# Weighting attention probabilities in the transpose: diagonal matrices in place of gate transposes, and a mask on row pairs

## The chip, the cores and the metric

The kernel runs on one core of one Trainium2 chip. The metric is device time in microseconds, from runs of the whole program. The core has five engines that work from queues of their own: PE (TensorE: matrix products; its weight loads are listed as PEld), DVE (VectorE), ACT (ScalarE), POOL (GpSimd) and SP, which here issues DMAs. Matrix products are written to PSUM, eight banks of 128 partitions by 512 f32 numbers; all else lies in SBUF.

## The reference, cut to what matters

Two blocks, one after the other. The first is a linear attention with polynomial features (4 batches, 4 heads, 1088 positions, head size 32). Its output, with the heads side by side, is `x` of the second: 4 batches of 1088 rows of 128 numbers. The second is a mixture of four attention experts, and the change lies there:

```python
logits = x @ w_gate                       # four experts per row
topk = np.argpartition(-logits, 2)[:2]    # the two best; w = softmax over these two
for e in range(4):
    q, k, v = x @ wq[e], x @ wk[e], x @ wv[e]          # 64 columns each
    scores = where(causal, -1e9, q @ k.T / 8)
    a = exp(scores - scores.max(-1)); a /= a.sum(-1) + 1e-9
    ye = a @ v @ wo[e]
    out += (w of this row for expert e, or 0) * ye
```

Everything is computed in f32. All four experts are computed for all rows; the gate `w` is zero for the two that a row does not choose. So a row of an expert's `a` is multiplied by two numbers, its gate and one over its sum of exponentials, and it makes no difference in the result whether that is done to `a` or to `a @ v`.

## The kernel before

**Tiling.** Keys and queries are cut into blocks of 128 rows (eight, and a ninth of 64). Experts go in pairs `g` (two). A *unit* is one block of queries `i`, one batch `b` and one pair `g`: 8 x 2 x 4 = 64 units, and four more of kind "L" for the last 64 rows of each batch, which hold both pairs at once. Two units with neighbouring blocks ("A" and "B", x = 0 and 1) share one tile of transposed weights `aT` and one product with the values.

**One unit**, in the order of its data:

1. `scores` (L367; `scores_last`, L393): PE forms q k^T for both experts of the pair in two groups of 64 array rows (L379), and adds the causal mask on the last 128 columns by a bf16 product of the identity with a mask matrix (L382; in the last unit L412). DVE takes the row maximum (L386 for up to 512 keys, both experts in one instruction; else L389, one each). ACT takes the exponential into the tile `a` and sums it into `z` (`soften`, L364).
2. `turns_of` (L427): PE transposes `a` block by block against the f32 identity (L434), four blocks to one PSUM bank `tp`, and `evacuate` (L67) copies the bank into `aT`: every third evacuation on DVE (L70), the others on ACT (L72). The blocks come in the order of keys, with the two experts next to each other.
3. `gates` (L443): DVE adds 1e-9 to the sums and takes the reciprocal (L446, L447); POOL multiplies by the gate and spreads the product over 64 columns for each expert, `rb` (L450); PE transposes `rb` (L457) into `rt`, and ACT copies that into `rs` (L459). This is done for two units together.
4. `values` (L491; L519 in the last unit): PE multiplies `aT` by the values (L497, L526); DVE multiplies the result by `rs` on its way from PSUM into `yT` (L499, L528).
5. `output` (L535): PE multiplies `yT` by `wo` (L540), the result is evacuated, and SP writes it out.

**What sets the order.** PE's order is written out by hand: everything from L548 on is traced under a manual schedule of that one engine. The driver at the end of the function goes through the units. The work of a unit that waits for ACT is put off: after the scores of a unit come the transposes of the unit before (`jobs`), then pieces of the preparation of the next batch (`fill`, given out by `spend`), and then, where a unit has more than two banks of transposes, the first half of its own; its other banks become `jobs` of the next unit. The gate turn goes into the jobs of an "A" unit, the values behind the scores of a "B" unit, the output into the jobs of a later unit. On DVE, ACT, POOL and SP the order is left to a planner that takes instructions by readiness and order of tracing.

**Preparation.** `prepare` (L193) makes a batch's `x`, the projections of queries, keys and values, and the gates `gw` (the last 64 rows also as `gw8`). Constants are made at the start: the identity `ident` on POOL, its bf16 copy `identb` on DVE (L169), the mask `cmask` on POOL (L171).

**PSUM.** Four of the eight banks belong to the scores (two tiles `sc` of two banks); the other four turn round under the tag `tp`: transposes, values, gate turns, output and all of the preparation.

Of the kernel before, what the change touches and what calls it, by code (L numbers as in the profile page):

```python
# [19 lines left out]
def kernel(  # L20
# [46 lines left out]
    def evacuate(out_, in_):  # L67
        turn[0] += 1
        if turn[0] % 3 == 0:
            nc.vector.tensor_copy(out_, in_)  # L70
        else:
            nc.scalar.copy(out_, in_)  # L72
# [95 lines left out]
    identb = const("identb", [128, 128], BF16)  # L168
    nc.vector.tensor_copy(identb, ident)  # L169
    cmask = const("cmask", [128, 128], BF16)  # L170
    make_causal_mask(nc, cmask, mask_val=-1e30)  # L171
# [195 lines left out]
    def scores(b, i, g, qk, z):  # L367

        n = 128 * i + 128
        if n <= 512:  # L370
            t = ps_sc.tile([128, 2, 512], F32, tag="sc", name=f"sc{b}_{i}_{g}")
            sc = [t[:, e, :] for e in range(2)]
        else:
            sc = [ps_sc.tile([128, 1024], F32, tag="sc", name=f"sc{b}_{i}_{g}_{e}") for e in range(2)]
        for c0 in range(0, n, 512):
            c1 = min(c0 + 512, n)
            for e in range(2):
                rows = slice(64 * e, 64 * e + 64)
                nc.tensor.matmul(sc[e][:, c0:c1], qk[rows, g, 128 * i : 128 * i + 128], qk[rows, NG + g, c0:c1],  # L379
                                 start=True, stop=(c1 < n))  # L380
        for e in range(2):
            nc.tensor.matmul(sc[e][:, 128 * i : n], identb, cmask, start=False, stop=True)  # L382
        mx = p4.tile([128, 2], F32, tag="mx", name=f"mx{b}_{i}_{g}")
        ats = [p4.tile([128, S], F32, tag="a", name=f"a{b}_{i}_{g}_{e}") for e in range(2)]
        if n <= 512:
            nc.vector.tensor_reduce(mx, t[:, :, 0:n], axis=AX.X, op=ALU.max, negate=True)  # L386
        for e in range(2):
            if n > 512:
                nc.vector.tensor_reduce(mx[:, e : e + 1], sc[e][:, 0:n], axis=AX.X, op=ALU.max, negate=True)  # L389
            soften(ats[e][:, 0:n], sc[e][:, 0:n], mx[:, e : e + 1], z[:, e : e + 1])  # L390
        return ats

    def scores_last(b, qk, z):  # L393
# [16 lines left out]
        for e in range(2):  # L410
            for g in range(NG):
                nc.tensor.matmul(ext[e][64 * g : 64 * g + 64], identb[:, 0:64], cmask[:, 0:64],  # L412
                                 start=False, stop=True)
        ats = []
        for e in range(2):
            mx, zz = (p4.tile([128, 2], F32, tag=t, name=f"{t}{b}_8_{e}") for t in ("mx", "zz"))
            nc.vector.tensor_reduce(mx[:, 0:1], sc[e], axis=AX.X, op=ALU.max, negate=True)
            nc.vector.tensor_reduce(mx[:, 1:2], ext[e], axis=AX.X, op=ALU.max, negate=True)
            nc.vector.tensor_tensor(out=mx[:, 0:1], in0=mx[:, 0:1], in1=mx[:, 1:2], op=ALU.min)
            a = p4.tile([128, S], F32, tag="a", name=f"a{b}_8_{e}")  # L420
            soften(a[:, 0:1024], sc[e], mx[:, 0:1], zz[:, 0:1])
            soften(a[:, 1024:], ext[e], mx[:, 0:1], zz[:, 1:2])
            nc.vector.tensor_tensor(out=z[:, e : e + 1], in0=zz[:, 0:1], in1=zz[:, 1:2], op=ALU.add)
            ats.append(a)
        return ats

    def turns_of(name, i, ats, aT, q0):  # L427

        def some(k0, k1):
            tp = ps_tp.tile([128, 4, 128], F32, tag="tp", name=f"tp{name}_{k0}")  # L430
            nk = size(k0 // 2)
            for k in range(k0, k1):
                j, e = divmod(k, 2)
                nc.tensor.transpose(tp[0:nk, k - k0, :], ats[e][:, 128 * j : 128 * j + nk], ident)  # L434
            evacuate(aT[0:nk, k0:k1, q0 : q0 + 128], tp[0:nk, 0 : k1 - k0, :])

        full = 2 * min(i + 1, NJ - 1)
        cuts = [(k, min(k + 4, full)) for k in range(0, full, 4)]
        if i == NJ - 1:
            cuts.append((full, full + 2))  # L440
        return [lambda k0=k0, k1=k1: some(k0, k1) for k0, k1 in cuts]

    def gates(name, z, gws, w):  # L443

        r = p4.tile([128, w // 128, 2], F32, tag="r", name=f"r{name}")
        nc.vector.tensor_scalar_add(r, z, 1e-9)  # L446
        nc.vector.reciprocal(r, r)  # L447
        rb = p4.tile([128, 2, 128], F32, tag="rb", name=f"rb{name}", bufs=2)
        wide = [128, w // 128, 2, HD]
        nc.gpsimd.tensor_tensor(out=rb[:, 0 : w // 128].rearrange("p x (e d) -> p x e d", d=HD),  # L450
                                in0=gws[:, :, :, None].to_broadcast(wide), in1=r[:, :, :, None].to_broadcast(wide),
                                op=ALU.mult)

        def turn():
            t = ps_tp.tile([128, 512], F32, tag="tp", name=f"rt{name}")
            for x in range(w // 128):
                nc.tensor.transpose(t[:, 128 * x : 128 * x + 128], rb[:, x], ident)  # L457
            rs = p4.tile([128, 256], F32, tag="rs", name=f"rs{name}", bufs=2)
            nc.scalar.copy(rs[:, 0:w], t[:, 0:w])  # L459
            return rs  # L460

        return turn
# [16 lines left out]
    def units(b, qk, vt, gw, gw8):  # L479


        for p in range((NJ - 1) // 2) if b < B - 1 else reversed(range((NJ - 1) // 2)):
            yT = p2.tile([128, NG, 256], F32, tag="yT", name=f"yT{b}_{p}")
            nk = 2 * (2 * p + 2)
            for g in range(NG):
                aT = p2.tile([128, 16 * 256], F32, tag="aT", name=f"aT{b}_{p}_{g}")
                aT = aT[:, 0 : nk * 256].rearrange("p (k s) -> p k s", s=256)
                z = p4.tile([128, 2, 2], F32, tag="z", name=f"z{b}_{p}_{g}")
                name = f"{b}_{p}_{g}"

                def values(rs, p=p, g=g, aT=aT, yT=yT, name=name):  # L491
                    av = ps_tp.tile([128, 512], F32, tag="tp", name=f"av{name}")
                    for j in range(2 * p + 2):
                        lo = 128 * max(0, j - 2 * p)
                        for e in range(2):
                            c = HD * (2 * g + e)
                            nc.tensor.matmul(av[HD * e : HD * e + HD, lo:256], vt[:, j, c : c + HD],  # L497
                                             aT[:, 2 * j + e, lo:256], start=(j == 0), stop=(j == 2 * p + 1))
                    nc.vector.tensor_tensor(out=yT[:, g], in0=av[:, 0:256], in1=rs, op=ALU.mult)  # L499
                    return (lambda: output(b, p, yT)) if g == NG - 1 else None  # L500

                def close(p=p, g=g, z=z, name=name, values=values):
                    return gates(name, z, gw[:, 2 * p : 2 * p + 2, 2 * g : 2 * g + 2], 256), values

                for x in range(2):
                    i = 2 * p + x
                    yield ("AB"[x], lambda i=i, g=g, z=z, x=x: scores(b, i, g, qk, z[:, x]),
                           lambda ats, i=i, aT=aT, x=x, name=name: turns_of(f"{name}_{x}", i, ats, aT, 128 * x),
                           close if x else None)
# [3 lines left out]
    def last_unit(b, qk, vt, gw8):  # L513
        aT = p2.tile([128, 16 * 256], F32, tag="aT", name=f"aT{b}_8")
        aT = aT[:, 0 : 18 * 128].rearrange("p (k s) -> p k s", s=128)
        z = p4.tile([128, 1, 2], F32, tag="z", name=f"z{b}_8")
        yT = p2.tile([128, NG, 256], F32, tag="yT", name=f"yT{b}_8")

        def values(rs):  # L519
            av = ps_tp.tile([128, 512], F32, tag="tp", name=f"av{b}_8")  # L520
            for g in range(NG):
                for j in range(NJ):
                    m = size(j)
                    for e in range(2):
                        c = HD * (2 * g + e)
                        nc.tensor.matmul(av[HD * e : HD * e + HD, 64 * g : 64 * g + 64], vt[0:m, j, c : c + HD],  # L526
                                         aT[0:m, 2 * j + e, 64 * g : 64 * g + 64], start=(j == 0), stop=(j == NJ - 1))
            nc.vector.tensor_tensor(out=yT[:, :, 0:64], in0=av[:, 0:128].rearrange("p (g s) -> p g s", g=NG),  # L528
                                    in1=rs[:, 0:128].rearrange("p (g s) -> p g s", g=NG), op=ALU.mult)
            return lambda: output(b, NJ // 2, yT)  # L530

        return ("L", lambda: scores_last(b, qk, z[:, 0]), lambda ats: turns_of(f"{b}_8", NJ - 1, ats, aT, 0),
                lambda: (gates(f"{b}_8", z, gw8[:, None, :], 128), values))
# [14 lines left out]
    with tc.manual_schedule(engines={mybir.EngineType.PE}):  # L548
# [10 lines left out]
        for b in range(B):  # L559
# [4 lines left out]
            for n, (kind, make, turned, close) in enumerate(units(b, *now)):  # L564
# [4 lines left out]
                if group and kind != "B":  # L569
                    to_gate, values = group  # L570

                    def gate_turn(to_gate=to_gate, values=values):
                        rs = to_gate()
                        return lambda: values(rs)

                    if kind == "A":
                        box = []
                        jobs.append(lambda gate_turn=gate_turn, box=box: box.append(gate_turn()))
                if kind == "L":
                    for f in jobs:  # L580
                        f()
                    values = gate_turn()
                    ats = make()
                    done = values()
# [3 lines left out]
                else:  # L588
                    ats = make()
# [9 lines left out]
                    if kind == "A" and group:  # L599
                        group = box[0]  # L600
                if n == 0 and b == 0:
                    while len(fill) > need + 5:
# [4 lines left out]
                turns = turned(ats)  # L607
# [4 lines left out]
                if close:  # L612
                    group = close()
# [4 lines left out]
        to_gate, values = group  # L618
        for f in turns + ([done] if done else []):
            f()  # L620
        values(to_gate())()
# [30 lines left out]
```

## Time and profile before

| | |
|---|---|
| median of three runs | 418.97 us (418.88 to 420.64) |
| the profiled execution | 420.57 us, of which the profile's span is 418.7 us |
| granted clock of PE | 0.995 of full speed |
| busy: PE / DVE / ACT / POOL | 396.7 / 232.1 / 224.9 / 55.9 us |
| records of PE / DVE / ACT / POOL | 3284 / 496 / 564 / 84 |
| first product of the preparation starts | 9.52 us |
| last evacuation (L72, `ob`) starts | 415.40 us |

A row of the groups reads: line, engine, operation, what it writes <- what it reads, the shapes, the number of records, and behind the bar the time in which at least one of them ran, the mean duration of one, and the engine's idle time just before them with what ended it. Matmuls are pipelined, so the durations of neighbours overlap: the mean duration is not the time from one to the next. For a matmul the shape gives the weights first (array rows * columns) and then what streams past them. A row of the timeline reads: start, length, engine, line, operation, tiles, shape and count of a burst. The idle time of an engine that does not bound the kernel costs nothing.

### The profile page before, as it was taken

Reading aid. Unit: us, or ns where it says so; the run is one execution under the profiler, and the core shown is the slowest. Engines: PE = TensorE matmul, PEld = TensorE weight load, DVE = VectorE, ACT = ScalarE, POOL = GpSimd, SP = SyncE. Lnnn points to the kernel's source line nnn. Section 1 sums busy time; section 2 is a strip of 40 time slices with the busy share of each in tenths; the row PEclk is TensorE's granted clock in tenths of the full one; section 3 lists DMA queues with packets and bytes.
Section 4 is the critical chain, followed back from the end, with each engine's and each line's share of the span. In section 5 each row is a group of like instructions: output and inputs, shape, how many; then the busy total and the mean of one; then the engine's idle time right before and its main releaser. Section 6 shows DMA issues by size and latency. Waiting matters only on the chain.

```text
span 418.7 us, 8188 instructions
## 1 busy us (share of the span) xinstructions
PE 396.7 (95%) x3284; PEld 274.1 (65%) x3284; DVE 232.1 (55%) x496; ACT 224.9 (54%) x564; POOL 55.9 (13%) x84
## 2 busy tenths in 40 slices
PE   5989999999999999998999999999999998999995
PEld 5965777865666766775765776786666565576663
DVE  5775756754854464656447345556575545545552
ACT  1325565655546464555745555575455655455662
POOL 2200460000000361000000063000000000000110
PEclk9989999999999999999999999999999999999999
DMA  8631032000000000000000000000000000000000
GB/s 201 170 104 58 0 112 65 6 8 2 13 3 15 5 0 14 2 14 0 15 1 2 14 3 14 2 12 2 2 13 2 0 14 5 2 14 4 2 13 28
DMA packets 11351, 9.98 MB, mean 24 GB/s; under 512 B 3632, under 2 KB 10288, under 8 KB 11312
## 3 DMA queue, kind: packets, MB, share of 16 engines
q1 hardware_dynamic: 9296, 8.92, 7.5%
q10 hardware_dynamic: 2016, 0.53, 0.7%
q8 instruction: 26, 0.43, 0.4%
q14 instruction: 13, 0.11, 0.1%
HBM read 7.22 MB, written 2.23 MB: 23 GB/s over the span
## 4 chain that ended last, share of the span: by engine, by line
PE 80%; ACT 9%; DVE 6%; issue 3%; DMA 1%; POOL 0%; POOLq 0%; ACTq 0%; DVEq 0%
PE sc L379 18%; PE tp L434 15%; PE av L497 14%; PE qk L304 7%; ACT a L365 6%; PE sc L382 3%; PE po L540 3%; PE num L277 3%; PE kps L229 2%; PE vg L316 2%; PE kv L255 2%; PE av L526 2%; PE tq L268 2%; PE sc L402 2%; DVE mx L389 2%
## 5 line engine op out<-in xcount | busy, mean ns | idle before, releaser
L365 ACT ACTIVATE a<-sc,mx 128x1024 f32<-128x1024 f32 (+7 forms) x136 | 103.0, 762 | 86.7 <-DVE mx L389 48.2
L434 PE MATMUL tp<-ident,a 128*128 128x128 f32 (+1 forms) x648 | 95.1, 278 | 6.3 <-ACT a L365 4.8
L389 DVE TENSOR_REDUCE mx<-sc 128x1 f32<-128x640 f32 (+3 forms) x64 | 62.6, 1019 | 49.0 <-PE sc L382 49.0
L72 ACT COPY aT<-tp 128x512 f32<-128x512 f32 (+1 forms) x122 | 63.1, 539 | 45.6 <-PE tp L434 45.2
L434 PEld LDWEIGHTS tp<-ident,a 128*128 128x128 f32 (+1 forms) x648 | 71.3, 140 | 22.4 <-ACT a L365 9.7
L379 PE MATMUL sc<-qkT 64*128 64x512 f32 (+3 forms) x384 | 80.9, 518 | 0.8 <-ACT a L365 0.8
L497 PE MATMUL av<-aT,vt 128*64 128x256 f32 (+1 forms) x640 | 69.2, 363 | 0.0
L450 POOL TENSOR_TENSOR rb<-gw,r 128x256 f32<-128x256 f32 (+1 forms) x36 | 21.2, 589 | 322.9 <-DVE r L447 258.2
L497 PEld LDWEIGHTS av<-aT,vt 128*64 128x64 f32 x640 | 42.9, 137 | 21.7 <-issue 0.2
L379 PEld LDWEIGHTS sc<-qkT 64*128 64x128 f32 x384 | 32.2, 185 | 31.3 <-issue 26.2
L70 DVE COPY aT<-tp 128x512 f32<-128x512 f32 (+2 forms) x58 | 37.7, 652 | 16.2 <-PE tp L434 15.7
L386 DVE TENSOR_REDUCE mx<-sc 128x2 f32<-128x256 f32 (+3 forms) x32 | 26.2, 819 | 19.7 <-PE sc L382 19.7
L304 PE MATMUL qk<-xT,wqk 128*128 128x512 f32 x64 | 33.0, 633 | 1.0 <-ACT xT L72 0.9
L365 ACT ACTIVATION_READ_ACCUMULATOR a<-sc,mx 128x1 f32 x136 | 27.1, 199 | 0.0
L382 PEld LDWEIGHTS <-identb 128*128 128x128 bf16 x128 | 7.3, 97 | 28.1 <-issue 26.2
L316 PE MATMUL vg<-wvg,xT 128*128 128x260 f32 (+1 forms) x72 | 21.4, 396 | 1.1 <-DVE vt L70 0.5
L540 PE MATMUL po<-wo,yT 128*128 128x128 f32 (+1 forms) x144 | 20.5, 282 | 1.7 <-ACT aT L72 0.8
L499 DVE TENSOR_TENSOR yT<-av,rs 128x256 f32<-128x256 f32 x32 | 13.5, 422 | 13.9 <-PE av L497 13.7
L540 PEld LDWEIGHTS po<-wo,yT 128*128 128x128 f32 (+1 forms) x144 | 17.5, 185 | 3.5 <-ACT aT L72 1.1
L382 PE MATMUL sc<-cmask,identb 128*128 128x128 bf16 x128 | 18.3, 224 | 0.0
L304 PEld LDWEIGHTS qk<-xT,wqk 128*128 128x128 f32 x64 | 11.1, 199 | 10.2 <-issue 5.9
L277 PE MATMUL num<-kvz,qpT 128*128 128x66 f32 x144 | 17.4, 271 | 0.0
(118 smaller groups left out, 402.3 us busy)
## 6 DMA issues: line engine op xcount, KB each, us to landing
kin<-in_k_dram SPq DMA_DIRECT2D x4, 544.0 KB, 3.7
qin<-in_q_dram SPq DMA_DIRECT2D x4, 544.0 KB, 5.5
vin<-in_v_dram SPq DMA_DIRECT2D x16, 128.0 KB, 3.4
out_dram<-ob SPq DMA_DIRECT2D x16, 128.0 KB, 1.8
wqk<-in_moe_wq_dram ACTq DMA_DIRECT2D x1, 128.0 KB, 4.3
wqk<-in_moe_wk_dram ACTq DMA_DIRECT2D x1, 128.0 KB, 6.6
wvg<-in_moe_wv_dram ACTq DMA_DIRECT2D x1, 128.0 KB, 6.8
wo<-in_moe_wo_dram ACTq DMA_DIRECT2D x1, 128.0 KB, 6.0
```

The costliest lines, as they stand in the source:

```text
L70: nc.vector.tensor_copy(out_, in_)
L72: nc.scalar.copy(out_, in_)
L277: nc.tensor.matmul(num[:, 66 * y : 66 * y + 66], qpT[:, 6 * g + y], kvz[:, y % 2].rearrange("p h d -> p (h d)"), start=True, stop=True)
L304: nc.tensor.matmul(t, wt(a), xT[:, 512 * c : 512 * c + 512], start=True, stop=True)
L316: nc.tensor.matmul(t[0:m, 0 : E * HD + E], xT[:, 128 * j : 128 * j + m], wvg, start=True, stop=True)
L365: nc.scalar.activation(out=dst, in_=src, func=ACTF.Exp, bias=mx, accum_out=z)
L379: nc.tensor.matmul(sc[e][:, c0:c1], qk[rows, g, 128 * i : 128 * i + 128], qk[rows, NG + g, c0:c1], start=True, stop=(c1 < n))
L382: nc.tensor.matmul(sc[e][:, 128 * i : n], identb, cmask, start=False, stop=True)
L389: nc.vector.tensor_reduce(mx[:, e : e + 1], sc[e][:, 0:n], axis=AX.X, op=ALU.max, negate=True)
L434: nc.tensor.transpose(tp[0:nk, k - k0, :], ats[e][:, 128 * j : 128 * j + nk], ident)
L497: nc.tensor.matmul(av[HD * e : HD * e + HD, lo:256], vt[:, j, c : c + HD], aT[:, 2 * j + e, lo:256], start=(j == 0), stop=(j == 2 * p + 1))
L540: nc.tensor.matmul(po[0:nq, DM * x : DM * x + DM], yT[:, g, 128 * x : 128 * x + nq], wo_sb[:, g], start=(g == 0), stop=(g == NG - 1))
```

## The change

- The weights `a` are no longer transposed against the identity, but multiplied, as stationary operand, by a diagonal matrix `dg` (f32, 128x128, one for each expert of a unit) with gate over sum on the diagonal. The result is the transposed and already weighted `a`. `nc.tensor.transpose` becomes `nc.tensor.matmul`.
- `weigh` makes these matrices on DVE: 1e-9 is added to the sums, the reciprocal taken, and the identity scaled by reciprocal and gate. In units with more than 512 keys and in the last unit that is done for each expert by itself, behind its exponential; in the others for both at once, when the transposes are begun.
- `gates` is dropped, and with it the broadcast on POOL, the transposes of `rb` and the copies to `rs`. `values` ends with a plain copy on ACT.
- A PSUM bank of transposes now holds blocks of one expert (for five and six blocks one bank holds the remainders of both), and `aT` is laid out by expert first.
- The mask is added in two halves of 64 columns by products over 64 array rows, a pair for the two experts: `mrows` holds a triangle of 64 rows, and `mpick` picks a row of it for each query.
- Every fourth instead of every third evacuation goes to DVE; in the first batch the loop over `fill` stops at need + 3 instead of need + 5.

```diff
     def evacuate(out_, in_):
         turn[0] += 1
-        if turn[0] % 3 == 0:
+        if turn[0] % 4 == 0:
...
-    identb = const("identb", [128, 128], BF16)
-    nc.vector.tensor_copy(identb, ident)
-    cmask = const("cmask", [128, 128], BF16)
-    make_causal_mask(nc, cmask, mask_val=-1e30)
+    mrows = const("mrows", [128, 64], BF16)
+    mpick = const("mpick", [128, 2, 128], BF16)
+    nc.gpsimd.memset(mrows, 0.0)
+    nc.gpsimd.memset(mpick, 0.0)
+    for e in range(2):
+        rows = slice(64 * e, 64 * e + 64)
+        for out_, cols, base, keep, fill in (
+            (mrows[rows], 64, 0, ALU.is_gt, -1e30),
+            (mpick[rows, 0], 128, -1, ALU.not_equal, 1.0),
+            (mpick[rows, 1, 64:], 64, -1, ALU.not_equal, 1.0)):
+            nc.gpsimd.affine_select(out=out_, in_=out_, compare_op=keep, fill=fill,
+                                    base=base, pattern=[[-1, cols]], channel_multiplier=1)
+        nc.gpsimd.memset(mpick[64 * e : 64 * e + 1, 1, 0:64], 1.0)
...
+    def sums(name):
+        z = p4.tile([128, 2], F32, tag="z", name=f"z{name}")
+        return z, p4.tile([128, 2, 128], F32, tag="dg", name=f"dg{name}", bufs=3)
+
+    def weigh(dg, z, gws, e0, e1):
+        nc.vector.tensor_scalar_add(z[:, e0:e1], z[:, e0:e1], 1e-9)
+        nc.vector.reciprocal(z[:, e0:e1], z[:, e0:e1])
+        for e in range(e0, e1):
+            nc.vector.tensor_scalar(out=dg[:, e], in0=ident, scalar1=z[:, e : e + 1], scalar2=gws[:, e : e + 1],
+                                    op0=ALU.mult, op1=ALU.mult)
...
-        for e in range(2):
-            nc.tensor.matmul(sc[e][:, 128 * i : n], identb, cmask, start=False, stop=True)
+        for half in range(2):
+            for e in range(2):
+                rows = slice(64 * e, 64 * e + 64)
+                c0 = 128 * i + 64 * half
+                nc.tensor.matmul(sc[e][:, c0 : c0 + 64], mpick[rows, half], mrows[rows], start=False, stop=(half == 1))
...
             soften(ats[e][:, 0:n], sc[e][:, 0:n], mx[:, e : e + 1], z[:, e : e + 1])
-        return ats
+            if n > 512:
+                weigh(dg, z, gws, e, e + 1)
+        return ats, dg, (lambda: weigh(dg, z, gws, 0, 2)) if n <= 512 else None
...
-        def some(k0, k1):
-            tp = ps_tp.tile([128, 4, 128], F32, tag="tp", name=f"tp{name}_{k0}")
-            nk = size(k0 // 2)
-            for k in range(k0, k1):
-                j, e = divmod(k, 2)
-                nc.tensor.transpose(tp[0:nk, k - k0, :], ats[e][:, 128 * j : 128 * j + nk], ident)
-            evacuate(aT[0:nk, k0:k1, q0 : q0 + 128], tp[0:nk, 0 : k1 - k0, :])
-
-        full = 2 * min(i + 1, NJ - 1)
-        cuts = [(k, min(k + 4, full)) for k in range(0, full, 4)]
+        def some(e0, e1, j0, j1):
+            tp = ps_tp.tile([128, 512], F32, tag="tp", name=f"tp{name}_{e0}_{j0}")
+            nk, nj = size(j0), j1 - j0
+            for e in range(e0, e1):
+                for j in range(j0, j1):
+                    x = nj * (e - e0) + j - j0
+                    nc.tensor.matmul(tp[0:nk, 128 * x : 128 * x + 128], ats[e][:, 128 * j : 128 * j + nk], dg[:, e],
+                                     start=True, stop=True)
+            evacuate(...)
+        n = min(i + 1, NJ - 1)
+        if n <= 2:
+            cuts = [(0, 2, 0, n)]
+        elif n <= 4:
+            cuts = [(0, 1, 0, n), (1, 2, 0, n)]
+        elif n <= 6:
+            cuts = [(0, 1, 0, 4), (0, 2, 4, n), (1, 2, 0, 4)]
+        else:
+            cuts = [(0, 1, 0, 4), (0, 1, 4, n), (1, 2, 0, 4), (1, 2, 4, n)]
...
-                    nc.vector.tensor_tensor(out=yT[:, g], in0=av[:, 0:256], in1=rs, op=ALU.mult)
+                    nc.scalar.copy(yT[:, g], av[:, 0:256])
...
-                    while len(fill) > need + 5:
+                    while len(fill) > need + 3:
```

`gates` and its calls in the driver are deleted; the last unit (`scores_last`, `last_unit`) is changed in the same way.

## The prediction

> **What bounds the kernel now.** I read the page's first part, its chain and its costliest groups; then the groups kept apart by shape; then the timeline of short stretches, to count matmul records against the calls in the code.
>
> ```profile
> PE 396.7 (95%) x3284; PEld 274.1 (65%) x3284; DVE 232.1 (55%) x496; ACT 224.9 (54%) x564; POOL 55.9 (13%) x84
> PE 80%; ACT 9%; DVE 6%; issue 3%; DMA 1%; POOL 0%; POOLq 0%; ACTq 0%; DVEq 0%
> ```
>
> TensorE (PE) is busy 95% of the span and makes 80% of the chain that ended last. VectorE (DVE) and ScalarE (ACT) stand still almost half of the time. So a change counts by what it does to PE's stream of matmuls, and work on DVE or ACT counts only where PE has to wait for it. PE's idle time is 418.7 - 396.7 = 22.0 us.
>
> ```profile
> L434 PE MATMUL tp<-ident,a 128*128 128x128 f32 x640 | 93.9, 278 | 6.3 <-ACT a L365 4.8 <-DVE xs L284 0.5 <-DVE aT L70 0.4
> L540 PE MATMUL po<-wo,yT 128*128 128x128 f32 x128 | 17.9, 281 | 1.7 <-ACT aT L72 0.8 <-DVE yT L499 0.5 <-DVE aT L70 0.2
> L457 PE MATMUL rt<-ident,rb 128*128 128x128 f32 x68 | 13.6, 277 | 0.9 <-POOL rb L450 0.7
> L382 PE MATMUL sc<-cmask,identb 128*128 128x128 bf16 x128 | 18.3, 224 | 0.0
> ```
>
> Line 434 holds the transposes of the attention weights. Line 540 is an ordinary f32 matmul of the same shape: 128x128 stationary, 128 columns moving. By the column of mean durations the two cost the same, 278 and 281 ns, and one would call the exchange of the one for the other free. But the durations overlap, and the counts say something else. Lines 434 and 441 ask for 162 transposes per batch, 648 in all, and the page counts 648 records at L434. Lines 538 to 541 ask for 18 matmuls per batch, 72 in all, and the page counts 144. Every other f32 matmul is doubled too: 10 calls at line 552 make 20 records, 32 projections at line 304 make 64. The transposes (also L268, L294, L457) and the bf16 mask matmuls (64 x 2 = 128) have one record per call. The timeline of PE shows it in one place:
>
> ```profile
> 406.37 0.28 PE L382 MATMUL sc<-cmask,identb 128*128 128x128 bf16 x2
> 406.49 0.61 PE L434 MATMUL tp<-ident,a 128*128 128x128 f32 x4
> 406.93 1.06 PE L540 MATMUL po<-wo,yT 128*128 128x128 f32 x8
> 407.83 0.38 PE L457 MATMUL rt<-ident,rb 128*128 128x128 f32 x2
> ```
>
> Four transposes hold the stream from 406.49 to 406.93, where the next burst starts: 0.44 us, 0.110 each. The eight records after them are one call of the output projection, two blocks by two groups, so four matmuls: 406.93 to 407.83, 0.90 us, 0.225 each. An f32 matmul takes two passes, a transpose one.
>
> **The change part by part.**
>
> Transposes become matmuls. Each of the 648 transposes against the identity becomes an f32 matmul of the same 128x128 weights against an f32 diagonal matrix. I take the price of the row with the same operands' shapes and types, L540, in a longer run of the timeline:
>
> ```profile
> 205.17 1.05 PE L540 MATMUL po<-wo,yT 128*128 128x128 f32 x8
> 207.93 1.04 PE L434 MATMUL tp<-ident,a 128*128 128x128 f32 x8
> ```
>
> Start to start, a record takes (1.05 - 0.275)/7 = 0.111 us at L540 and (1.04 - 0.272)/7 = 0.110 us at L434. So a transpose goes from 0.110 to 0.222 us, and 648 x 0.112 = **+72.6 us**, all of it on the engine that is the bound. That a diagonal is nearly all zeros takes nothing off: the matmuls of line 552 have the identity on both sides and still have two records. Ends: 0 if these matmuls went in one pass, +72.6 otherwise; I take the second, by the row.
>
> The Trainium skill, "TensorE: Matmul & The Clock Gate", section Terms, says that on trn2 the transpose mode is four times faster for FP32; this trace has a factor of 2.0 (0.222 against 0.110). By the page's factor the step would cost an estimated 648 x 3 x 0.110 = 214 us and the kernel would end near 616 us; the measured factor decides.
>
> Gate transposes and their surroundings go. 68 transposes of `rb` at 0.110 = **-7.5 us** on PE, and with them PE's wait for POOL, **-0.7 us** (the row of L457). The 36 copies of `rs` on ACT (12.4 us for 32 of them) go, and 36 copies of `yT` come in their place; the multiplications of `yT` leave DVE (13.5 us for 32). On ACT the copy stands in line behind exponentials of 1.1 us; the output projection that reads it comes only in the next unit's work, so I cost it at nothing; uncovered it would be 36 x about 0.4 = 14 us at most.
>
> Diagonals on DVE. Lines with up to 512 keys: 32 units with one addition and one reciprocal; longer ones and the last rows: 36 units with two of each. That is 104 x (0.170 + 0.173, rows of L446 and L447) = 35.7 us, and 136 scalings of 128x128, for which the nearest row is the 128x256 scaling at the start (0.29 us): at most 39 us, about 27 with 0.2 each. Gone are the 36 pairs of L446/L447 (about 12 us), the `yT` products (about 15) and, with every fourth instead of every third evacuation, some 10 us. DVE ends near 232 + 63 - 37 = 258 us, 54% of a longer span. What counts is the delay: after the sum of an exponential is read, DVE's chain runs 0.21 (addition to reciprocal, start to start) + 0.21 + 0.2 and PE hears of it, about 0.8 us later than before. Long units gain it back: the banks hold one expert each, so the first waits for one exponential (about 1.0 us of ACT less) and not for two. Short units wait for both. There the cover is what PE has between the exponentials and the transposes, which are put behind the next unit's scores; the doubled transposes of the unit before lengthen it by 0.2 to 0.9 us. I take **+1.5 us** for all of it; between 0 and +10 (32 short units x 0.3).
>
> Stalls that the longer PE stream covers. Of PE's 22.0 us idle, 4.9 lie before the first sketch matmul (9.52 us) and 3.3 behind the last (415.38); of the 13.8 between, 4.8 are transposes waiting for an exponential and most of the rest matmuls waiting for a bank to be emptied. With 0.45 us more PE work per bank, both come late less often. Ends 0 and -13.8; I take half, **-7 us**. ACT's larger share of the evacuations is hidden in the same way: 15 copies x 0.59 = 9 us on an engine with 45% idle.
>
> Mask. Two bf16 matmuls of 128 rows and 128 columns become four of 64 rows and 64 columns, in pairs on two row groups. Before: 406.37 to 406.49, 0.12 us per unit. If a pair runs side by side at the old row's rate, 4 x 64 columns take 0.05 to 0.11 us; if they run one after the other with their loads, 4 x 0.054 = 0.22. I take 0.11, 64 x -0.01 = **-0.6 us**; ends -4.5 and +6.4. The change of row grouping is a second term: before, the mask starts about 0.09 us late behind the 64-row scores (last score matmul from 202.87, 384 columns at 0.84 ns, so 203.19; the mask's first at 203.29). Now mask and scores share their rows, and the gap comes behind the mask instead. Where values with 64-column tiles follow (half of the units), that gap is there today as well: 32 x 0.09 = **-2.9 us**; ends -2.9 and 0.
>
> Start and end. POOL builds six masks by selection in place of one: 6 x 0.29 - 0.29, and two fills, +1.6 us, between its copies of the sketch matrices and its last fills (9.47 us), just before PE's first sketch matmul. DVE's copies of the same matrices end at 9.37, so either may be what PE waits for. I take 0; ends 0 and +1.6. At the end POOL's product (0.65) and the `rt` turn (0.44) leave the chain, but the two scalings (0.4) and the second pass of four transposes (0.45) enter it, and the evacuation is no longer hidden beside the gates (0.6): **+0.5 us**.
>
> Sum: 72.6 - 7.5 - 0.7 + 1.5 - 7 - 0.6 - 2.9 + 0.5 = +55.9 us. On the profiled execution, 418.7 us of span in 420.57, that makes 474.6 and 476.5. The median of the runs is 418.97, 1.6 below the profiled one: **475 us**.
>
> **The rivals.**
>
> *One pass.* If a matmul against the diagonal cost what a transpose costs, the first term falls away, and the covers with it: -7.5 - 0.7 - 0.6 - 2.9 + 5 (delays of the diagonals, now uncovered) + 0.5, about 413 us, faster. It decides as soon as the new step stays below 0.13 us per matmul. For it speaks nothing but the equal mean durations; against it every f32 matmul in the page. Chance 0.04.
>
> *Half hidden.* The second pass could overlap with its neighbours, for the load is the same kind for both: some 0.165 us per matmul, about 440 us. L540's burst, the same shapes, shows no such thing. Chance 0.04.
>
> *DVE becomes late.* DVE works in order. Were a diagonal's addition put ahead of the next maximum, or an evacuation, while its exponential still ran, DVE would stand for up to 1.1 us in each of the 36 long units, and maxima, exponentials and transposes after it. A third to a half of that reaching PE, with the relief lost: 475 + 7 + 12 to 20, 494 to 502 us. Against it: DVE's share of about 54%, and today's maxima of the two experts run back to back. Chance 0.09.
>
> **How the numbers follow.** Forecast 0.80, DVE late 0.09, one pass 0.04, half hidden 0.04, something else 0.03. The forecast's ends: all idle time covered, mask at its best and nothing late, 475 - 6.8 - 3.9 - 1.5 = 463; no relief but half, a serial mask and the slower start, 475 + 3.5 + 7 + 1.6 + 2 = 489. The range 463 to 489 holds nearly the whole of the forecast and little else, about 8 in 10. A measurement of this kernel tells about 0.5% from no change. Slower 0.95, same 0.01, faster 0.04.
>
> **What would show it.** Right: the new line of the transposes has 1296 f32 records, not 648, at 0.111 us start to start, and PE's records rise by 648 - 68 + 128, to about 3990. PE stays over 95% busy, DVE near 258 us, ACT near 234. Waits of transposes, now for DVE's diagonals, stay under 8 us. Mask: 256 records and no gap ahead of them. Wrong: 648 records there; or twice as many at well under 0.1 us; or a row in which PE waits for the diagonal with 20 us or more.

## The result and the profile after

The changed kernel takes 495.94 us (495.5 to 498.73) against 419.3 us: ratio 1.184, 95% interval 1.178 to 1.189. The direction was forecast; the size was not: 475 us with a range of 463 to 489, so the loss is 76.6 us where 56 were expected.

The first lines of the page of the changed kernel, and its costliest groups (busy us, mean ns of one | PE's or DVE's idle time before them):

```profile
span 494.3 us, 9783 instructions
PE 457.9 (93%) x3992; PEld 355.4 (72%) x3992; DVE 269.2 (54%) x706; ACT 242.6 (49%) x589; POOL 36.9 (7%) x56
PE 83%; DVE 10%; ACT 3%; issue 2%; DMA 1%; ACTq 0%; DVEq 0%
L475 PE MATMUL tp<-dg,a 128*128 128x128 f32 x1296 | 174.4, 283 | 20.0 <-DVE dg L389 16.5
L389 DVE TENSOR_SCALAR dg<-ident,z,gw 128x128 f32<-128x128 f32 x136 | 48.8, 376 | 3.3
```

Two things are seen at once. The line of the transposes has 1296 records and 174.4 us busy where it had 648 and 95.1, and PE's records are 3992: the second pass is there (a pass is here one record of the profile per call; what the array does within a record no run shows), and PE's busy time rose by 457.9 - 396.7 = 61.2 us, close to what the forecast's terms on PE's stream add up to (72.6 - 7.5 - 0.6 - 2.9 = 61.6; the four kernels below show that this closeness is partly luck). But PE's idle time did not shrink from 22.0 us, as was forecast, it grew to 36.4, and the page names the new releaser: `dg`, the diagonals, 16.5 us. The share of DVE in the chain that ended last went from 6% to 10%. Two of the signs that the forecast named for being right fail by this page: PE is busy 93% and not over 95%, and the waits for diagonals are 16.5 us and not under 8.

One of those waits, in the timeline of the changed kernel (start, length, engine, line, operation, tiles, shape, count, idle time before and what ended it):

```profile
51.20 0.23 PE L410 MATMUL sc<-mrows,mpick 64*128 64x64 bf16 x4
54.14 2.05 PE L475 MATMUL tp<-dg,a 128*128 128x128 f32 x8 [2.72 <-DVE dg L389]
...
50.14 0.17 DVE L386 TENSOR_SCALAR z<-z 128x2 f32<-128x2 f32 x1 [1.40 <-ACT a L378]
50.34 1.25 DVE L226 STREAM_TRANSPOSE kT<-kin 128x1024 f32<-128x1024 f32 x1
51.51 0.51 DVE L248 TENSOR_TENSOR kab<-kab,kps 128x256 f32<-128x256 f32 x2
51.94 0.15 DVE L387 RECIPROCAL z<-z 128x2 f32<-128x2 f32 x1
52.01 0.94 DVE L415 TENSOR_REDUCE mx<-sc 128x2 f32<-128x768 f32 x1
52.87 1.71 DVE L389 TENSOR_SCALAR dg<-ident,z,gw 128x128 f32<-128x128 f32 x2
...
51.97 2.53 POOL L252 TENSOR_TENSOR kp<-kab 128x1024 f32<-128x1024 f32 x2 [1.80 <-DVE kab L248]
```

The sums of a short unit are ready at 50.14. Between the addition and the reciprocal DVE does preparation of the next batch (`kT`, `kab`, 1.7 us); between the reciprocal and the diagonals it does the next unit's maximum (0.94 us); and the two diagonals take 1.71 us instead of about 0.6 while POOL is at work. PE, which went through the next unit's scores in the meantime, stands for 2.7 us. Waits for diagonals of 1.7 to 2.7 us like this one end at 41, 54, 65, 174, 185 and 298 us, in the short units with which a batch begins.

### The profile page after: what moved, and what is told of

Its sections match the earlier page's. It is cut to its first block, busy times and chain, and to the rows that moved or that the text cites. A ratio compares the mean times of both kernels' runs of the same rounds, so it can differ in the third digit from the quotient of the medians.

```text
span 494.3 us, 9783 instructions
## 1 busy us (share of the span) xinstructions
PE 457.9 (93%) x3992; PEld 355.4 (72%) x3992; DVE 269.2 (54%) x706; ACT 242.6 (49%) x589; POOL 36.9 (7%) x56
## 4 chain that ended last, share of the span: by engine, by line
PE 83%; DVE 10%; ACT 3%; issue 2%; DMA 1%; ACTq 0%; DVEq 0%
PE tp L475 31%; PE sc L404 14%; PE av L525 11%; PE qk L317 5%; PE po L562 4%; ACT a L378 3%; PE num L290 3%; PE vg L329 3%; PE av L550 2%; PE kps L242 2%; DVE mx L450 2%; PE kv L268 2%; PE tq L281 2%; PE sc L433 2%; DVE dg L389 1%
## 5 line engine op out<-in xcount | busy, mean ns | idle before, releaser
L475 PE MATMUL tp<-dg,a 128*128 128x128 f32 x1296 | 174.4, 283 | 20.0 <-DVE dg L389 16.5
L475 PEld LDWEIGHTS tp<-dg,a 128*128 128x128 f32 x1296 | 156.6, 192 | 32.3 <-issue 12.0
L72 ACT COPY aT<-tp 128x512 f32<-128x512 f32 (+2 forms) x131 | 71.5, 548 | 67.8 <-PE tp L475 67.4
L389 DVE TENSOR_SCALAR dg<-ident,z,gw 128x128 f32<-128x128 f32 x136 | 48.8, 376 | 3.3
L70 DVE COPY aT<-tp 128x512 f32<-128x512 f32 (+3 forms) x49 | 30.4, 619 | 36.1 <-PE tp L475 35.4
L386 DVE TENSOR_SCALAR z<-z 128x1 f32<-128x1 f32 (+1 forms) x104 | 16.4, 157 | 39.1 <-ACT a L378 37.6
L317 PE MATMUL qk<-xT,wqk 128*128 128x512 f32 x64 | 30.4, 602 | 2.7 <-ACT a L378 1.5
L252 POOL TENSOR_TENSOR kp<-kab 128x1024 f32<-128x1024 f32 (+1 forms) x9 | 13.4, 1507 | 226.3 <-DVE kab L248 226.3
L410 PEld LDWEIGHTS <-mpick 64*128 64x128 bf16 x256 | 13.1, 94 | 17.0 <-issue 12.6
L72 ACT COPY qkT<-qk 128x512 f32<-128x512 f32 x25 | 14.6, 585 | 17.1 <-PE qk L317 17.0
```

The source lines that it names most:

```text
L317: nc.tensor.matmul(t, wt(a), xT[:, 512 * c : 512 * c + 512], start=True, stop=True)
L389: nc.vector.tensor_scalar(out=dg[:, e], in0=ident, scalar1=z[:, e : e + 1], scalar2=gws[:, e : e + 1], op0=ALU.mult, op1=ALU.mult)
L475: nc.tensor.matmul(tp[0:nk, 128 * x : 128 * x + 128], ats[e][:, 128 * j : 128 * j + nk], dg[:, e], start=True, stop=True)
```

## The experiments

The theory after the result: the second pass costs what was forecast, and the 21 us by which the forecast missed are waits for diagonals, made on DVE's queue. The rivals: the delays on DVE make most of the loss and the second pass little; or the new matmuls cost more than the row they were priced by. Four kernels make a table of two causes, two and two.

**One pass.** In `turns_of` and `weigh`:

```diff
-                    nc.tensor.matmul(tp[...], ats[e][...], dg[:, e], start=True, stop=True)
+                    nc.tensor.transpose(tp[...], ats[e][...], dg[:, e])
...
             nc.vector.tensor_scalar(out=dg[:, e], in0=ident, scalar1=z[:, e : e + 1], scalar2=gws[:, e : e + 1],
-                                    op0=ALU.mult, op1=ALU.mult)
+                                    op0=ALU.is_ge, op1=ALU.is_gt)
```

> The changed kernel, but the 648 products with the diagonals are transposes again, in one pass, against a matrix that DVE makes by the same chain (addition, reciprocal, a 128x128 two-scalar operation with sum and gate) and that comes out as the identity; so every wait for a diagonal stays, and the weighting by gate over sum is left out. Theory (the second pass makes the loss, 648 x 0.112 = 72.6 us, and the rest are waits for diagonals): 496 - 73 = 423 us, and up to 10 more, since a shorter PE stream covers less: 423 to 433 us, 648 records on the line of the transposes. Rival (the delays on DVE make most of the loss): above 450 us. The rival of the forecast that one pass would win: about 413 us.

Measured: 451.68 us, ratio 1.074 (1.070 to 1.078). The second pass is worth 44 us here and not 73, and what is left is some 31 us slower than before. The number lies far from the theory's 423 to 433 us and just inside the rival's range (above 450 us). Yet what the rival says, that the delays make most of the loss, does not follow from it: 44 of the 76 us went with the second pass. The other two corners of the table decide.

**No diagonals.** `weigh` does nothing, and the product is taken with `ident`:

```diff
     def weigh(dg, z, gws, e0, e1):
+        return
...
-                    nc.tensor.matmul(tp[...], ats[e][...], dg[:, e], start=True, stop=True)
+                    nc.tensor.matmul(tp[...], ats[e][...], ident, start=True, stop=True)
```

> The changed kernel, but the products go against the constant identity and DVE makes no diagonals; the weighting by gate over sum is left out. The second pass stays, every wait for a diagonal goes. Theory (the 21 us by which the forecast missed are waits for diagonals, 16.5 us on PE's row, with 2 to 4 us of slow clock behind the longest of them): 470 to 478 us. Rival (a matmul against a diagonal is dearer than the output projection's row, or something else in the change holds PE up): 488 us or more.

Measured: 473.57 us, ratio 1.126 (1.122 to 1.129). So the diagonals cost 22 us in the changed kernel, and without them it is within 1.5 us of the forecast. The price of a matmul was right: the page has the same 1296 records, and PE hardly waits.

```profile
PE 455.2 (96%) x3992; PEld 353.2 (75%) x3992; DVE 192.3 (41%) x362; ACT 240.5 (51%) x589; POOL 36.3 (8%) x56
L475 PE MATMUL tp<-ident,a 128*128 128x128 f32 x1296 | 172.4, 281 | 1.2 <-ACT a L378 1.2
```

**Neither.** The fourth corner: no diagonals, and transposes against `ident`.

> The fourth corner: the changed kernel without diagonals and with transposes against the constant identity in one pass; the weighting by gate over sum is left out. The other corners are 496 (both), 452 (diagonals alone) and 474 us (second pass alone). Theory (the two costs cover each other: the second pass costs its 72.6 us whole where nothing waits for a diagonal, and the diagonals cost some 45 to 50 us where PE's stream is short): 474 - 73 = 401 us, to 408 with the waits for exponentials that the shorter stream uncovers. Rival (the two add up, and the second pass is worth 44 us in this kernel whatever the diagonals do): 474 - 44 = 430 us.

Measured: 407.75 us, ratio 0.971 (0.967 to 0.974). The rival, that the two costs add up, falls: 430 us was its number. The four medians:

| | no diagonals | diagonals | cost of the diagonals |
|---|---|---|---|
| one pass | 407.8 | 451.7 | 43.9 |
| two passes | 473.6 | 495.9 | 22.4 |
| cost of the second pass | 65.8 | 44.3 | |

(These runs were made in groups, and the kernel before has medians of 419.3 to 420.7 us in them: a difference between groups is good to about 1.5 us.) Beside the second pass the diagonals cost half of what they cost without it. What their 44 us are made of is seen in the two kernels with one pass, which have the same number of matmul records, first the one with diagonals, then the one without:

```profile
PE 402.0 (89%) x3344; PEld 287.3 (64%) x3344; DVE 267.8 (59%) x706; ACT 237.9 (53%) x589; POOL 36.6 (8%) x56
L475 PE MATMUL tp<-dg,a 128*128 128x128 f32 (+1 forms) x648 | 98.9, 285 | 33.0 <-DVE dg L389 27.0 <-ACT a L378 2.9 <-DVE z L386 1.9
```

```profile
PE 383.0 (94%) x3344; PEld 276.4 (68%) x3344; DVE 192.4 (47%) x362; ACT 235.8 (58%) x589; POOL 36.8 (9%) x56
L475 PE MATMUL tp<-ident,a 128*128 128x128 f32 (+1 forms) x648 | 96.0, 280 | 6.7 <-ACT a L378 5.6 <-ACT aT L72 0.8 <-ACT yT L526 0.2
```

The spans are 450.5 and 406.2 us. Of the 44 us, 25 are idle time of PE (48.5 against 23.2) and 19 are a longer busy time for the same 3344 records: the mean granted clock is 0.945 against 0.994. With two passes the spans are 494.3 and 472.2 us, and the same split gives 19.4 us of idle time (36.4 against 17.0) and 2.7 of busy time (457.9 against 455.2). So the longer stream covers only some 6 us of the waiting. The other 16 us of the difference are busy time, and go with the clock, which with two passes is 0.986 and 0.989. What slows the clock is taken up in the last section.

**Why the diagonals come late.** The timeline shows three things in their way: the order on DVE, preparation included; the length of the chain; POOL. The next runs take them one by one. First the order, by tracing the four instructions of `weigh` under `tc.high_priority()`:

```diff
+        with tc.high_priority():
-        nc.vector.tensor_scalar_add(z[:, e0:e1], z[:, e0:e1], 1e-9)
+            nc.vector.tensor_scalar_add(z[:, e0:e1], z[:, e0:e1], 1e-9)
...
```

> The changed kernel with the four instructions of a diagonal traced at high priority, so that the planner puts them ahead of the next unit's maximum on DVE where they compete. Theory (DVE works in order, and a maximum that waits for the next unit's scores stands ahead of a diagonal that PE waits for): the waits of about 2 us in the units of 256 and 384 keys lose 1 to 1.3 us each, five or six of them, and the slow clock behind them: 484 to 491 us. Rival (the waits are the length of the chain and POOL's hold on DVE, not the order): 494 to 497 us.

Measured: 492.92 us, ratio 1.174 (1.169 to 1.178), so 3 us and between the two expectations. PE's wait for diagonals fell from 16.5 to 10.1 us, but PE now waits 2.4 us for `kab` and, at its weight loads, 3.2 us for `qab`, which the priority pushed back. (The loads of `qab` name ACT, L246.) Order is a part of the cause, and moving it makes others late.

**The form of the instruction.** POOL's work was suspected to hold back the two-scalar form alone:

```diff
-            nc.vector.tensor_scalar(out=dg[:, e], in0=ident, scalar1=z[...], scalar2=gws[...], op0=ALU.mult, op1=ALU.mult)
+            nc.vector.scalar_tensor_tensor(out=dg[:, e], in0=ident, scalar=z[...],
+                                           in1=gws[...].to_broadcast([128, 128]), op0=ALU.mult, op1=ALU.mult)
```

> The changed kernel with each diagonal made by a three-operand instruction (identity times sum, times the gate spread over 128 columns) in place of the two-scalar one; the order on DVE is the same. Theory (the two-scalar form has to stand back while POOL's products of the features run: 7 of 136 took 0.98 us on average, up to 2.06, against 0.34): no diagonal over 0.5 us, PE's waits for diagonals 3 to 5 us less: 490 to 493 us. Rival (the long ones are a matter of what else runs, not of the form): the long ones stay, 495 to 497 us.

Measured: 498.63 us, ratio 1.187 (1.182 to 1.192): no gain. The instructions on DVE and their order are the same, and the 7 of 136 diagonals that overlap POOL's work still take 1.03 us on average, up to 2.13. Whatever holds them back, it is not this form. With both mendings together:

> Both mendings of the diagonals together, high priority and the three-operand form. If order and form are separate causes, the gains add: 493 - 3 to 5, 487 to 490 us; if they are the same waits seen twice, 492 to 493 us.

Measured: 495.49 us, ratio 1.180 (1.174 to 1.186). Nothing is added; the form is no mending, and most of the gain of the order is gone. POOL does not tell the two kernels with priority apart, 16 diagonals meet its work in both. PE's idle time is even a little shorter here (32.2 us against 33.9); its busy time is longer (460.5 against 456.5), with one more stretch at half clock, at 175 us.

**POOL.** The products of the sketches are put on DVE:

```diff
-            (nc.vector if first else nc.gpsimd).tensor_tensor(
+            nc.vector.tensor_tensor(
```

> The changed kernel with the products of the sketches (18 of them from the second batch on, 1.95 us each on POOL for 1024 columns) on DVE, where the first batch has them already (1.22 us). Theory (POOL's products hold DVE's diagonals up): no diagonal above 0.5 us, against up to 2.06; but DVE gets some 19 us more in the same stretches, so the time stays within 3 us: 493 to 499 us. Rival (the long diagonals have another cause): some stay near 2 us.

Measured: 507.3 us, ratio 1.208 (1.205 to 1.211). The group of the diagonals in this kernel, and in the changed one (duration of one in ns: least, median, greatest):

```profile
L389 DVE TENSOR_SCALAR dg<-ident,z,gw x136: 274/346/349, 42.2 to 498.1; 128x128 f32<-128x128 f32 x136
```

```profile
L389 DVE TENSOR_SCALAR dg<-ident,z,gw x136: 276/346/2064, 41.1 to 485.3; 128x128 f32<-128x128 f32 x136
```

So it is POOL that makes the long diagonals. But they are not the main thing: with 16 us of products more on DVE, PE waits still more (20.7 us for diagonals, two waits of 3.6), and the kernel loses 11 us where at most 3 were expected. By the two pages 3 of these are idle time of PE (39.8 us against 36.4) and 8 are busy time (466.0 against 457.9), at a mean granted clock of 0.969 against 0.986. The Trainium skill, "SBUF — State Buffer", section "Who interferes with whom", says that a DVE instruction in a two-port mode, or with two inputs in SBUF against a GpSimd instruction that reads SBUF, shares a port pair with GpSimd, one of them blocked for the whole instruction. By the page both forms tried here can fall under that, the two-scalar one if it runs in a two-port mode, which no run here shows. The runs agree in size: up to 2.06 and 2.13 us beside POOL's products of 1.95 us, 0.35 without.

**A shorter chain.** A sum of exponentials is at least 1, so adding 1e-9 changes nothing in f32:

```diff
-        nc.vector.tensor_scalar_add(z[:, e0:e1], z[:, e0:e1], 1e-9)
```

> The changed kernel without the addition of 1e-9 to the sums (a sum is at least 1, so in f32 the addition changes nothing). The chain of a diagonal has two links instead of three, DVE has 104 instructions less (16 us), and on DVE's queue the diagonals of the units up to 512 keys now stand ahead of the next unit's maximum. Theory (short units wait for the chain and for the maximum put ahead of it): of PE's 16.5 us of waits for diagonals some 8 go, with the slow clock behind the longest: 484 to 489 us. Rival (the waits are made by the exponentials' place, the chain only comes last): 492 to 496 us.

Measured: 493.95 us, ratio 1.177 (1.173 to 1.182), as the rival had it. But not for the rival's reason. The order came out as said, the diagonals ahead of the next maximum; only now the two of the wait shown above begin with POOL's products and last as long as those:

```profile
51.50 0.17 DVE L386 RECIPROCAL z<-z 128x2 f32<-128x2 f32 x1 [1.40 <-ACT a L378]
51.70 1.25 DVE L226 STREAM_TRANSPOSE kT<-kin 128x1024 f32<-128x1024 f32 x1
52.87 0.51 DVE L248 TENSOR_TENSOR kab<-kab,kps 128x256 f32<-128x256 f32 x2
53.31 2.64 DVE L388 TENSOR_SCALAR dg<-ident,z,gw 128x128 f32<-128x128 f32 x2
53.33 2.53 POOL L252 TENSOR_TENSOR kp<-kab 128x1024 f32<-128x1024 f32 x2 [1.80 <-DVE kab L248]
55.51 0.84 PE L474 MATMUL tp<-dg,a 128*128 128x128 f32 x3 [2.72 <-DVE dg L388]
```

13 diagonals meet POOL instead of 7. One cause stepped into the place of another, and the wait is again 2.7 us. The shorter chain with priority:

> The same, with the links at high priority: the diagonals come ahead of the maximum and, where they compete, of the preparation of the next batch as well. If the high priority helps by order alone, which the shorter chain already gives, nothing more comes of it: within 2 us of the run without priority. If the preparation on DVE was the cause, 3 us less or more.

Measured: 484.39 us, ratio 1.152 (1.149 to 1.155), 9.6 us less than without priority: the preparation on DVE ahead of the diagonals was a cause, by itself or by what it starts on POOL. For ahead of `kab` the diagonals also come before POOL's products begin, and only 5 of them meet POOL's work. Against the changed kernel the waits that end at 54 and 174 us are down from 2.7 to 0.5 us, those at 65 and 185 from 1.9 to 0.7. This takes back 11.5 of the 22.4 us; what is left are the first wait of all (2.0 us, behind the gates of the first batch), two long units that wait 1.3 us each, and the end of the kernel (1.4 us), where nothing stands beside the chain.

**The mask alone**, on the kernel before:

```diff
-        for e in range(2):
-            nc.tensor.matmul(sc[e][:, 128 * i : n], identb, cmask, start=False, stop=True)
+        for half in range(2):
+            for e in range(2):
+                rows = slice(64 * e, 64 * e + 64)
+                c0 = 128 * i + 64 * half
+                nc.tensor.matmul(sc[e][:, c0 : c0 + 64], mpick[rows, half], mrows[rows], start=False, stop=(half == 1))
```

> The kernel before with the mask on row pairs alone. Theory of the forecast (32 gaps of 0.09 us saved in units followed by values, 64 x 0.01 us in the masks): 419.3 - 3.5, about 416 us. Rivals: the masks of a pair run one after the other, 0.1 us more each, 421 to 425 us; or the gap only moves and nothing is saved, 419 us.

Measured: 413.26 us, ratio 0.984 (0.980 to 0.988), a gain of some 6.7 us by the ratio, twice the forecast's 3.5. PE's timeline, kernel before and then this one, shows where a block's scores, its mask and what follows begin, once followed by transposes and once by values:

```profile
201.58 1.77 PE L379 MATMUL sc<-qkT 64*128 64x512 f32 x8
203.29 0.29 PE L382 MATMUL sc<-cmask,identb 128*128 128x128 bf16 x2
203.41 0.61 PE L434 MATMUL tp<-ident,a 128*128 128x128 f32 x4
...
208.90 1.99 PE L379 MATMUL sc<-qkT 64*128 64x512 f32 x8
210.82 0.28 PE L382 MATMUL sc<-cmask,identb 128*128 128x128 bf16 x2
211.03 1.30 PE L497 MATMUL av<-aT,vt 128*64 128x256 f32 x10
```

```profile
200.25 1.77 PE L389 MATMUL sc<-qkT 64*128 64x512 f32 x8
201.86 0.23 PE L395 MATMUL sc<-mrows,mpick 64*128 64x64 bf16 x4
202.01 0.66 PE L448 MATMUL tp<-ident,a 128*128 128x128 f32 x4
...
207.34 1.99 PE L389 MATMUL sc<-qkT 64*128 64x512 f32 x8
209.16 0.23 PE L395 MATMUL sc<-mrows,mpick 64*128 64x64 bf16 x4
209.31 1.95 PE L511 MATMUL av<-aT,vt 128*64 128x256 f32 x16
```

From the scores' start to the next burst: 1.83 us before and 1.76 now with transposes behind, 2.13 and 1.97 with values behind. That is 32 x 0.07 + 32 x 0.16 = 7.4 us. The gap ahead of the mask is gone, as forecast; the four half masks take about 0.06 us (in the trace the second pair starts 0.028 us behind the first) where 0.11 was assumed.

**Banks of one expert**, on top of the mask, with transposes and gates as before. `some` in `turns_of` and the layout of `aT` are those of the change, with `nc.tensor.transpose(..., ident)`.

> The kernel before with the mask on row pairs and with banks of one expert each, filled by transposes against the identity; gates as before. Theory (the first bank of a long unit then waits for one exponential instead of two; PE's wait for exponentials in the mask_pairs run is 5.0 us behind its row and 10.1 at its weight loads): 413.3 - 3 to 6, 407 to 411 us. Rival (those waits are hidden again by the next one): 413 us.

Measured: 411.29 us, ratio 0.979 (0.976 to 0.983). It beats both kernels. PE's wait of the transposes for exponentials fell from 5.0 us behind its row to 1.7 and from 10.1 at its weight loads to 4.1; 2 us of that reach the time, less than the 3 to 6 that were expected. With every fourth evacuation on DVE as well:

> The kernel before with the mask on row pairs, banks of one expert, and every fourth evacuation on DVE, all with transposes and gates as before. Theory (the smaller parts of the change are worth what they are without the diagonals; ACT evacuates 0.59 us against DVE's 0.69 and both stand idle half of the time): within 2 us of the 411 us without this part.

Measured: 411.22 us, ratio 0.979 (0.978 to 0.981): no difference.

## Why the prediction was wrong

- *Transposes become matmuls, +72.6 us: right.* The record counts are as forecast. With no diagonals to wait for, PE's busy time is 72.2 us longer with two passes than with one (455.2 against 383.0), and the second pass costs 65.8 us net of the idle time that it covers. The forecast had 72.6 - 7.0 = 65.6 for the two.
- *Gate transposes and mask: right in sum, by luck.* Forecast -7.5 - 0.7 - 0.6 - 2.9 = -11.7; the kernel with neither diagonals nor second pass stands 12.1 us below the kernel before (407.75 against 419.86). But of these 12.1 the mask and the banks of one expert make 8.6 (411.29 against 419.86), where 3.5 was forecast for the mask and the banks stood only as a cover for the diagonals. What is left for the gates is 3.5 us (407.75 against 411.29), where 8.2 was forecast. The closeness of PE's busy time, 61.2 against 61.6, is of the same kind: without diagonals it is 58.5, and the waits for diagonals add 2.7 by the slow clock.
- *Diagonals on DVE, +1.5 us, bounds 0 and +10: the step that failed.* They cost 22.4 us in this kernel, 19.4 of them idle time of PE. The step counted the chain's own links, 0.8 us, and set PE's cover against them. It did not ask what DVE's queue would put between the links: preparation of the next batch (1.7 us in the wait shown) and the next unit's maximum (0.94). A link was priced at 0.2 us by a guess under a 0.29 us row and took 0.35. And the products on POOL, visible in the profile before, were not weighed against DVE's new instructions at all. The mended kernels show the queue and POOL at work; how the 22.4 us split among them cannot be said, since taking one away put another in its place.
- *Stalls that the longer stream covers, -7 us:* borne out without diagonals (PE's idle time 17.0 us), overridden with them (36.4).
- *The rival "DVE becomes late", 494 to 502 us, chance 0.09,* has the right time and the right engine, but another place: it spoke of diagonals that block the next maximum in the long units. It is the other way round, and in short units: the maximum and the preparation stand ahead of diagonals that PE waits for. The long units do wait, 0.9 to 1.5 us three times (at 108 and 343 us the profile names the exponential, at 411 the diagonal), but that is the smaller part.
- *The rival "one pass", 413 us, faster,* would have been wrong by its own condition too: with one pass the kernel takes 451.7 us, since the term of 5 us for uncovered delays is 44.

## What to carry to other kernels

Count a trace's records against the calls in the code before pricing one operation by another: here the mean durations of a transpose and of an f32 matmul, 278 and 281 ns, hid that the matmul is two records, 0.222 us against 0.110. When a new step stands between two engines, price not its own instructions but the queue that it joins: what the in-order engine will do between its links, and what runs beside it on an engine that it disturbs. And causes that act on each other must be removed together as well as one by one: the diagonals cost 22 us beside the second pass and 44 without it. Then split each difference into idle and busy time of the bound engine before naming a reason: here most of the gap between 22 and 44 is not covered waiting but busy time at a slower clock.

## What the runs showed of the hardware

After the longest waits PE ran at half its clock, which no term of the forecast had. The stretches of the changed kernel behind the wait of 2.7 us (busy us and records of each engine, then PE's granted clock, DMA share and GB/s):

```profile
53.00:54.00 1.00, 0.00 (x0) 0.00 (x0) 1.00 (x2) 0.96 (x3) 1.00 (x2) 0.94 0.00 0
54.00:55.00 1.00, 0.86 (x4) 0.89 (x5) 0.95 (x4) 0.27 (x2) 0.49 (x1) 0.50 0.00 0
55.00:56.00 1.00, 1.00 (x7) 1.00 (x7) 0.60 (x2) 0.00 (x0) 0.00 (x0) 0.50 0.39 39
56.00:57.00 1.00, 1.00 (x6) 1.00 (x6) 0.00 (x0) 0.58 (x1) 0.00 (x0) 0.50 0.58 196
57.00:58.00 1.00, 1.00 (x10) 1.00 (x9) 0.00 (x0) 0.30 (x1) 0.00 (x0) 0.86 0.84 330
58.00:59.00 1.00, 1.00 (x7) 0.67 (x8) 0.42 (x2) 0.45 (x2) 0.39 (x1) 1.00 0.05 9
```

Half the clock for about 3 us, and twice the time per record: the eight records at 54.14 in the timeline above take 2.05 us, the eight that follow a shorter wait 1.13:

```profile
65.02 1.13 PE L475 MATMUL tp<-dg,a 128*128 128x128 f32 x8 [1.88 <-DVE dg L389]
```

In the changed kernel this followed both waits of 2.7 us and none of the single waits of 0.9 to 2.0 us but the one at the very end. In the kernel with one pass and diagonals it followed waits of 2.3 and 2.7 us in five of six cases, and there the slow clock is 19 of the 44 us. But it also followed waits of 1.6 to 1.9 us there, at 276, 431 and 442 us, so the length of a wait does not decide. In every trace of this case the stretches at half clock begin and end on a raster of 3.41 us (in the changed kernel at 53.88, 57.29, 173.34 and 176.76 us), and what counts is PE's idle time within one window of it. Two windows of the kernel with one pass, each with the next one (columns as above):

```profile
104.05:107.46 3.41, 1.77 (x11) 1.24 (x13) 2.04 (x8) 2.69 (x6) 0.00 (x0) 1.00 0.02 5
107.46:110.87 3.41, 3.41 (x32) 1.99 (x30) 2.21 (x2) 0.90 (x1) 0.00 (x0) 1.00 0.00 0
438.63:442.04 3.41, 1.51 (x18) 0.89 (x12) 1.88 (x7) 1.56 (x6) 0.00 (x0) 0.99 0.14 38
442.04:445.46 3.42, 2.75 (x14) 1.60 (x12) 0.00 (x0) 0.96 (x2) 0.00 (x0) 0.50 0.00 0
```

The wait of 2.30 us that ends at 106 us is parted by the raster, and 1.64 us of it fall into the first window shown: the clock stays. The wait of 1.90 us that ends at 442 us lies in one window: the clock falls. Over the 14 traces, from 12 us on, 30 windows have 1.65 us of idle time or more, and half clock follows all of them; between 1.40 and 1.65 us it follows 6 of 24, and below that no window that was not slow already. So a kernel can keep its clock with longer waits, if they fall well, and lose it with shorter ones. The Trainium skill, "TensorE: Matmul & The Clock Gate", section "Why this matters for your kernels", warns of idle gaps over about 3 us between bursts of matmuls; here 1.65 us within a window of 3.41 were enough. That the gaps cause the slow clock is read from their order in the traces; no run filled a gap to try it.
